# Window attention with a gated convolution: probabilities turned in half-height tiles, the last output block in two column halves, and a new order of the work

## The chip, the cores and the metric

The kernel runs on one core of one Trainium2 chip. A core has a matmul engine (TensorE, in the profile PE, with its weight loads apart as PEld), a vector engine (VectorE, DVE), a scalar engine (ScalarE, ACT), a general engine (GpSimd, POOL) and a queue engine (SyncE, SP) that issues most transfers. The metric is the device time of one execution in microseconds, smaller is better. A profile shows one execution; its span begins and ends with the traced instructions and is a little shorter than the time measured around it.

## The reference

Two layers follow each other. The first is attention with a window of 128 positions and 4 sink positions, on 4 batches, 8 heads, 768 positions and 64 channels per head, all in float32:

```
scores = q @ k.T / sqrt(64)                    # per batch and head, 768 x 768
keep   = (column < 4) | (0 <= row - column < 128)
a      = softmax(where(keep, scores, -1e9))
x      = a @ v                                 # heads put side by side: 4 x 768 x 512
```

The second is a gated convolution over the positions: `gate_pre` is a causal convolution of x with 5 taps per channel, `gate = 1 / (1 + exp(-gate_pre))`, `val = x @ w_val` and `out = (gate * val) @ w_out`, with 512 x 512 weights that arrive as 64-bit floats.

## The kernel before, in words

**Units of work.** The attention is cut into 24 steps. A step is one batch, one third of the positions (two blocks of 128 rows, `p` = 0, 1, 2) and half of the heads (`qd` = 0, 1: two pairs of heads, g = 0, 1, and in a pair the heads j = 0, 1). The second layer is cut into 12 units `m`: one batch and one third of the positions, with all 512 channels; unit m uses steps 2m and 2m+1.

**A step.** `scores` (s0, s1: one per pair of heads) multiplies q and k in 64x32 tiles of the matmul array, 16 matmuls that write a two-bank PSUM tile `pr`; `exps` and `recip` take the softmax, and `normalise` on POOL writes the normalised probabilities to `wx` and the sink columns to the block `skb`, in three parts (high, low, whole) next to each other. The window of a block of 64 queries lies in its own block of 64 keys and the two before it. Half 0 of `wx` ("x") holds the own and the farthest block in one, told apart by a mask when they are copied; half 1 ("y") holds the block between, which needs none. `probs_t` (tx) turns them with 8 transposes of 128x128 into a `pr` tile, a bank for each half; `probs_x` (px) on DVE and `probs_y` (py) on ACT copy them to `wt` in SBUF. `sinks_t` (sk) turns `skb` with one 128x128 transpose into an `ac` tile, `sinks_e` (ts) copies it. `values` (vl) multiplies v and `wt` in 64x64 tiles into `xv`, and `sinks` (si) adds the sinks with two matmuls of 128 rows and 256 columns, one for each pair of heads. There half of the weights `vh` are zero, since each pair's sinks stand in their own half of the rows. Then ACT copies x out (xc, xh), POOL takes the rest (xl) and the first tap (c4), DVE the other four taps (c0, c1), and ACT the tanh (th).

**A unit.** `val` (v0 to v3) is 12 matmuls of 256 columns each; `gated` (g, h, l) multiplies and splits the product in a high and a low part on DVE, ACT and POOL; `outp` (o0 to o3) is 6 matmuls of 512 columns each, two calls per block of 128 output rows; `store` (t0, t1) copies a block on ACT and sends it from SP. All of `val` and `outp` are 128x128 tiles of the array, as the transposes of before are.

**PSUM.** Two tiles `pr` of two banks are passed in turn to scores and turned probabilities, two banks `ac` ("homes") to weights, sinks, `val` and `outp`, and the two banks of `xv` to values.

**Order.** All instructions are issued in a hand-set order: the table `ORDER` names the calls one after the other (`tx.5` is `probs_t` of step 5), and each engine runs its instructions in that order, each held until its operands are there. The matmul engine is filled with work that has no use (`fill`) in the first part, where the weights are decoded from 64 bits (wva to wvf, woa to wof).

## Time and profile before

| | |
|---|---|
| median of 3 runs | 271.12 us (270.26 to 271.2) |
| the profiled execution | 270.55 us, span 268.7 us |
| busy PE / PEld | 258.3 us (96%) / 213.6 us (79%) |
| busy DVE / ACT / POOL | 205.4 (76%) / 189.1 (70%) / 176.2 us (66%) |
| moved by DMA | 36.93 MB, mean 137 GB/s |
| granted PE clock | 0.991 of full speed |

The busy time of an engine is the union of its instructions. A matmul's record is longer than the time for which it keeps the next one waiting, since matmuls run into each other in the array: the distance of two starts is what counts. A float32 matmul that isn't a transpose is recorded as two (`L391 x32` is the 16 matmuls of one `scores` call). Lines are those of the kernel before: L391 scores, L449 turned probabilities, L454 turned sinks, L504 values, L511 sinks, L566 `val`, L606 `outp`.

### The profile page before, as it was taken

The numbers are of one execution on the slowest core, as the hardware profiler recorded it, in microseconds if no ns is written. First come the engines' busy times: TensorE is split into PE (matmuls) and PEld (weight loads), VectorE is DVE, ScalarE is ACT, GpSimd is POOL, SyncE is SP. The second block draws the span as 40 slices with busy tenths as digits, with TensorE's granted clock in tenths as the row PEclk, the third lists the DMA queues.
The fourth block names the chain that finished last, engine by engine and source line by source line (L and its number), as shares of the span: only waits on it lengthen the run. The fifth ranks groups of instructions, "written<-read, shape, count | busy, mean of one in ns | idle before, by whom it ended". The sixth has DMA issues, their size and how long they took to land.

```text
span 268.7 us, 9474 instructions
## 1 busy us (share of the span) xinstructions
PE 258.3 (96%) x3760; PEld 213.6 (79%) x3760; DVE 205.4 (76%) x561; ACT 189.1 (70%) x667; POOL 176.2 (66%) x233
## 2 busy tenths in 40 slices
PE   7899999999999999999999999999999999999990
PEld 3356578789879888879879889889879889898970
DVE  6977989979869878998778788889478857834530
ACT  3899998897888867857676778968567757442420
POOL 6187986876948785675669464895776774816330
PEclk9999999999999999999999999999999999999996
DMA  7998633039344043318833619053335211040202
GB/s 220 370 384 267 239 105 104 0 112 348 107 133 168 1 158 120 131 40 290 262 115 98 196 66 305 3 146 115 111 132 201 59 44 40 1 139 2 78 14 75
DMA packets 27394, 36.93 MB, mean 137 GB/s; under 512 B 2256, under 2 KB 23760, under 8 KB 27344
## 3 DMA queue, kind: packets, MB, share of 16 engines
q1 hardware_dynamic: 26528, 35.48, 39.9%
...
q8 instruction: 31, 0.51, 0.8%
q14 instruction: 19, 0.16, 0.2%
...
## 4 chain that ended last, share of the span: by engine, by line
PE 83%; ACT 9%; POOL 2%; DMA 2%; issue 1%; DVE 0%; POOLq 0%; ACTq 0%
PE ac L606 25%; PE ac L566 25%; PE xv L504 11%; PE pr L391 10%; PE pr L449 7%; ACT w L416 4%; PE xv L511 3%; DMA raw<-in_w_val_dram 2%; PE ac L454 1%; POOL xl L534 1%; ACT wvh L151 1%; ACT wv_p L137 1%; ACT wv_p L156 1%; ACT wvl L183 1%; POOL wo_f L157 0%
## 5 line engine op out<-in xcount | busy, mean ns | idle before, releaser
L547 DVE SCALAR_TENSOR_TENSOR sg<-xv,cw,sg 128x256 f32<-128x256 f32 x192 | 77.8, 474 | 12.4 <-POOL sg L539 7.0
L431 POOL TENSOR_TENSOR wx<-w,sm 128x512 f32<-128x512 f32 x48 | 49.1, 1044 | 11.3 <-DVE sm L423 11.1
L416 ACT ACTIVATE w<-pr,ngm 128x132 f32<-128x132 f32 x136 | 48.5, 369 | 1.7
L595 POOL TENSOR_TENSOR gl<-sg,gh 128x512 fp32r<-128x512 f32 x24 | 31.0, 1295 | 28.1 <-ACT gh L591 28.0
L566 PE MATMUL ac<-xh,wvh 128*128 128x256 f32 x192 | 48.4, 286 | 0.0
L566 PE MATMUL ac<-xh,wvl 128*128 128x256 f32 x192 | 47.1, 279 | 0.0
L606 PE MATMUL ac<-woh,gh 128*128 128x512 f32 x96 | 39.2, 408 | 0.0
L539 POOL TENSOR_TENSOR sg<-xt,cw 128x512 f32<-128x512 f32 x24 | 25.0, 1043 | 20.6 <-ACT xt L518 20.6
L606 PE MATMUL ac<-wol,gh 128*128 128x512 f32 x96 | 38.0, 396 | 0.0
L606 PE MATMUL ac<-woh,gl 128*128 128x512 f32 x96 | 38.0, 395 | 0.0
L566 PEld LDWEIGHTS ac<-xh,wvh 128*128 128x128 f32 x192 | 36.1, 188 | 0.8 <-issue 0.5
L566 PEld LDWEIGHTS ac<-xh,wvl 128*128 128x128 f32 x192 | 36.2, 188 | 0.2
L391 PE MATMUL pr<-k,q 64*32 64x168 f32 x1536 | 35.3, 307 | 0.7 <-DMA q<-in_qt_dram 0.6
L504 PEld LDWEIGHTS xv<-wt,v 64*64 64x64 f32 x1024 | 30.4, 133 | 7.0 <-issue 4.5
L504 PE MATMUL xv<-wt,v 64*64 64x192 f32 (+2 forms) x1024 | 34.5, 278 | 0.2 <-PE ac L566 0.2
L534 POOL TENSOR_TENSOR xl<-xt,xh 128x512 fp32r<-128x512 f32 x24 | 30.8, 1289 | 3.2 <-ACT xh L526 2.8
L566 PE MATMUL ac<-xl,wvh 128*128 128x256 f32 x192 | 30.7, 280 | 0.4 <-POOL xl L534 0.4
L391 PEld LDWEIGHTS pr<-k,q 64*32 64x32 f32 x1536 | 23.8, 106 | 7.9 <-issue 2.6
L396 DVE COPY_PREDICATED pr<-low,pr 128x256 f32<-128x256 uint8 x48 | 20.3, 423 | 12.2 <-PE pr L391 12.2
L591 ACT ACTIVATE gh<-sg 128x512 fp32r<-128x512 f32 x24 | 15.0, 628 | 19.2 <-DVE sg L585 19.2
L416 ACT ACTIVATION_READ_ACCUMULATOR w<-pr,ngm 128x1 f32 x136 | 27.6, 203 | 0.0
L518 ACT ACTIVATE xt<-xv 128x512 f32<-128x512 f32 x24 | 14.4, 600 | 17.3 <-PE xv L511 17.2
...
## 6 DMA issues: line engine op xcount, KB each, us to landing
k<-in_kt_dram SPq DMA_DIRECT2D x23, 408.0 KB, 5.2
v<-in_vt_dram SPq DMA_DIRECT2D x16, 384.0 KB, 4.5
out_dram<-osb SPq DMA_DIRECT2D x24, 256.0 KB, 2.2
q<-in_qt_dram SPq DMA_DIRECT2D x23, 256.0 KB, 5.4
...
v<-in_vt_dram SPq DMA_DIRECT2D x8, 256.0 KB, 5.2
...
```

The costliest lines, as they stand in the source:

```text
L391: nc.tensor.matmul(ss[e * QB:(e + 1) * QB, j, c * n + x0:c * n + x1], q[js, g, (4 * c + e) * QB:(4 * c + e + 1) * QB], k[js, g, (2 * c + e ...
L396: nc.vector.copy_predicated(sv[:, :, :, :D], low[:, None, None, :].to_broadcast([P, 2, 2, D]), sv[:, :, :, 2 * HB:])
L416: nc.scalar.activation(out=w[:, g, j, c], in_=sx[:, j, c, :PK], func=AF.Exp, scale=0.125 if whole else -1.0, bias=ngm[:, g, j, c:c + 1], a ...
L431: nc.gpsimd.tensor_tensor(out=t[:, n].rearrange("p c h x -> p h c x"), in0=w[:, :, :, at], in1=sm.to_broadcast([P, 4, 2, D]), op=ALU.mult)
L449: nc.tensor.transpose(out=x[:, n, o:o + P], identity=ident, in_=ws[s][:, n, c, 2 * g:2 * g + 2].rearrange("p j x -> p (j x)"))
L504: nc.tensor.matmul(acc[o * D:(o + 1) * D, g, x0 + h * D:x0 + (h + a1 - a0 + 1) * D], v[js, g, n], t[js, g, n, a0:a1 + 1].rearrange("p a r ...
L534: nc.gpsimd.tensor_tensor(out=half(xls, s, "xl", F32R), in0=xts[s], in1=half(xhs, s, "xh", F32R).bitcast(F32), op=ALU.subtract)
L539: nc.gpsimd.tensor_tensor(out=half(sg, s, "sg", F32), in0=xts[s], op=ALU.mult, in1=cw[:, g, KT - 1:].to_broadcast([P, 2, PQ]))
L547: nc.vector.scalar_tensor_tensor(out=g, in0=x, scalar=a, in1=g, op0=ALU.mult, op1=ALU.add)
L566: nc.tensor.matmul(acc[:, h], a[:, kc, cs], x[:, kc], start=(n == 0), stop=(n == 11))
L595: nc.gpsimd.tensor_tensor(out=gl, in0=g, in1=gh.bitcast(F32), op=ALU.subtract)
L606: nc.tensor.matmul(acc, a[:, kc, ts], x[:, kc], start=(kc + n == 0), stop=(kc + n == 5))
```

## The change

The transposes of the probabilities are cut in two: each half of the 128 query rows (r = 0, 1) is turned by itself, as 64 rows by 128 columns against a 64x64 identity, and the two halves write different banks. That makes 16 transposes of 64 columns where 8 of 128 stood. `wt` is laid out anew, `probs_y` becomes two ACT instructions (one for each r, 256 elements per partition, or 128 and 256 where p = 0) in place of one of 512 (384), and `probs_x` keeps two DVE instructions of the same size.

The sinks of the two pairs now stand in different halves of `skb`'s columns, 16 for each part, so that `sinks` is two matmuls of 64 rows and 128 columns, one in each half of the array, each to its own bank. The weights `vsk`/`vh` lose their zero half: 64 KB a load in place of 128 KB, and a conversion of 128 elements in place of 256. The subtraction on POOL becomes two of 16 partitions and 128 elements.

In unit 11 the second block of 128 output rows is made in two halves of 256 columns (24 matmuls of 256 in place of 12 of 512), each copied and sent by itself, the first half while the second is being made, in another bank. For units 10 and 11 `outp` collects in a `pr` tile, except for that very last half. `ORDER` is a new table throughout.

```diff
-NR = 8 * NSK
+NR = 4 * NSK
@@ ORDER
-g0.11 th.23 g1.11 h0.11 l0.11 o2.11 h1.11 l1.11 o0.11 o1.11 flag t0.11 o3.11 t1.11
+g0.11 h0.11 l0.11 v3.11 g1.11 h1.11 l1.11 o1.10 t0.10 o0.11 o1.11 o3.10 t0.11 t1.10 flag o2.11 o3.11 t1.11
...
+MP = 10
+LAST = (B * NP - 1, 1)
@@ sink_values
-        vs[b, qd] = h = p2.tile([P, 2, P], F32R, name="vh", tag="vh", bufs=3)
+        vs[b, qd] = h = p2.tile([P, P], F32R, name="vh", tag="vh", bufs=3)
         nc.scalar.activation(out=h, in_=x, func=AF.Copy)
-        r = slice(2 * NR, 3 * NR)
-        nc.gpsimd.tensor_tensor(out=h[r], in0=x[r], in1=h[r].bitcast(F32), op=ALU.subtract)
+        for g in range(2):
+            r = slice(g * D + 2 * NR, g * D + 3 * NR)
+            nc.gpsimd.tensor_tensor(out=h[r], in0=x[r], in1=h[r].bitcast(F32), op=ALU.subtract)
@@ probs_t
-                    o = (2 * g + c) * P
-                    nc.tensor.transpose(out=x[:, n, o:o + P], identity=ident,
-                                        in_=ws[s][:, n, c, 2 * g:2 * g + 2].rearrange("p j x -> p (j x)"))
+                    for r in range(2):
+                        rs, o = slice(r * D, (r + 1) * D), (4 * n + 2 * c + g) * D
+                        nc.tensor.transpose(out=x[:, r, o:o + D], identity=ident[rs, rs],
+                                            in_=ws[s][rs, n, c, 2 * g:2 * g + 2].rearrange("p j x -> p (j x)"))
@@ probs_y
-        nc.scalar.activation(out=t[:, :, 1 + h0:5, 1], in_=x[:, :, h0:], func=AF.Copy)
+        for r in range(2):
+            c = 1 if steps[s][1] + r == 0 else 0
+            nc.scalar.activation(out=t[:, 1 - r, r + c:r + 2, :, 1].rearrange("p k g d -> p (k g) d"),
+                                 in_=x[:, r, 2 * c:], func=AF.Copy)
@@ sinks
         for g in range(2):
-            nc.tensor.matmul(accs[s][:, g, KT - 1:], vs[b, qd][:, g],
-                             skt[s].rearrange("p c r -> p (c r)"), start=False, stop=True, skip_group_check=True)
+            gs = slice(g * D, (g + 1) * D)
+            nc.tensor.matmul(accs[s][:, g, KT - 1:], vs[b, qd][gs], skt[s][gs].rearrange("p c r -> p (c r)"),
+                             start=False, stop=True, skip_group_check=True)
@@ outp
+        if m >= MP:
+            if m not in outs:
+                outs[m] = pair()
+            vacc[m, 2 + i] = outs[m][:, i]
...
+        if (m, i) == LAST:
+            if h:
+                piece(m, i, 0)
+                vacc[m, 2 + i] = acc = homes.pop(0)
+            cs = slice(h * PQ, (h + 1) * PQ)
+            for kc in range(4):
+                for n, (a, x) in enumerate(((gh, wh), (gh, wl), (gl, wh))):
+                    nc.tensor.matmul(acc[:, cs], a[:, kc, ts], x[:, kc, cs], start=(kc + n == 0), stop=(kc + n == 5))
+            return
...
+    def piece(m, i, h):
+        if h == 0:
+            obs[m, i] = p2.tile([P, DM], F32, name="osb", tag="osb", bufs=3)
+        cs = slice(h * PQ, (h + 1) * PQ)
+        nc.scalar.activation(out=obs[m, i][:, cs], in_=vacc[m, 2 + i][:, cs], func=AF.Copy, scale=0.5)
+        at = (2 * (m % NP) + i) * P
+        nc.sync.dma_start(out=out[m // NP, at:at + P, cs], in_=obs[m, i][:, cs])
```

Three places show what the change does to the order. The first is on the matmul engine, at the values of step 5, between two blocks of `outp` and the next scores. Before:

```order
L606 MATMUL ac_92<-wol,gh 128x512
L606 MATMUL ac_92<-woh,gl 128x512
L454 MATMUL ac_93<-ident,skb_108 128x128
L449 MATMUL pr_87<-ident,wx 128x128 x8
L504 MATMUL xv<-wt,v 64x64 x4
L504 MATMUL xv<-wt,v 64x128 x4
L504 MATMUL xv<-wt,v 64x192 x8
L504 MATMUL xv<-wt,v 64x128 x4
L504 MATMUL xv<-wt,v 64x64 x4
L511 MATMUL xv<-skt,vh 128x256 x2
L391 MATMUL pr_86<-k,q 32x168 x16
```

Now (L628 is `outp`, L462 the turned sinks, L454 the turned probabilities, L512 values, L520 sinks, L394 scores):

```order
L628 MATMUL ac_93<-wol,gh 128x512
L628 MATMUL ac_93<-woh,gl 128x512
L462 MATMUL ac_92<-ident,skb_108 128x128
L454 MATMUL pr_87<-ident,wx 128x64 x16
L512 MATMUL xv<-wt,v 64x64 x4
L512 MATMUL xv<-wt,v 64x128 x4
L512 MATMUL xv<-wt,v 64x192 x8
L512 MATMUL xv<-wt,v 64x128 x4
L512 MATMUL xv<-wt,v 64x64 x4
L520 MATMUL xv<-skt,vh 128x256 x2
L394 MATMUL pr_86<-k,q 32x168 x16
```

The sequence of work is the same; the transposes and the sinks have another shape of array tile than `outp` before them, than the values between them, and than the scores behind.

The second is a little later on the same engine, where turned probabilities stand inside a run of `val`. Before:

```order
L566 MATMUL ac_92<-xh,wvl 128x256
L566 MATMUL ac_92<-xl,wvh 128x256 x4
L449 MATMUL pr_86<-ident,wx 128x128 x8
L566 MATMUL ac_93<-xh,wvh 128x256
L566 MATMUL ac_93<-xh,wvl 128x256
```

Now (L575 is `val`):

```order
L575 MATMUL ac_93<-xh,wvl 128x256
L575 MATMUL ac_93<-xl,wvh 128x256 x4
L454 MATMUL pr_86<-ident,wx 128x64 x16
L575 MATMUL ac_92<-xh,wvh 128x256
L575 MATMUL ac_92<-xh,wvl 128x256
```

A run of one tile shape throughout has become three runs.

The third is on POOL in the first part, around the sink values of the first step (`vh`), the decoding of `w_out` (`wo_f`) and the second step's normalisation. Before:

```order
L438 TENSOR_TENSOR skb_107<-skb_107 128x32
L157 TENSOR_TENSOR wo_f<-wo_e,wo_p 128x512
L259 TENSOR_TENSOR vh<-vs,vh 32x256
L431 TENSOR_TENSOR wx<-w,sm 128x4x2x64 x2
L434 TENSOR_TENSOR skb_108<-w,sm 128x32
```

Now:

```order
L442 TENSOR_TENSOR skb_107<-skb_107 128x2x16
L262 TENSOR_TENSOR vh<-vs,vh 16x128 x2
L159 TENSOR_TENSOR wo_f<-wo_e,wo_p 128x512
L434 TENSOR_TENSOR wx<-w,sm 128x4x2x64 x2
L438 TENSOR_TENSOR skb_108<-w,sm 128x2x16
```

The sink values are two instructions and stand ahead of the decoding; the rest keeps its place.

More of the change, by code (lines that the diff above doesn't have):

```diff
@@ L77 @@
-ts.23 v2.10 v3.10 g0.10 c4.22 hd.22 c0.22 c1.22 th.21 g1.10 h0.10 l0.10 o2.10 vv.23 vl.23 h1.10 si.23 xc.23
-hd.23 xh.23 l1.10 xl.22 o0.10 o1.10 c4.23 c0.23 xl.23 t0.10 c1.23 o3.10 v0.11 th.22 v1.11 t1.10 v2.11 v3.11
-g0.11 th.23 g1.11 h0.11 l0.11 o2.11 h1.11 l1.11 o0.11 o1.11 flag t0.11 o3.11 t1.11
+fill.5 masks load_conv wvl.0 kq.0 signs leads conv_weights wva.0 wvb.0 wvd.0 s0.0 wvc.0 wvl.1 wva.1 wvl.2
+blanks e0.0 s1.0 wva.2 e1.0 wvb.1 wvc.1 fill.10 wve.0 wvf.0 wvb.2 wvc.2 kq.1 s1.1 wol.0 rec.0 norm.0 kq.2 e1.1
@@ new lines @@
+wvd.1 vv.0 woa.0 s0.1 e0.1 fill.7 wvl.3 s1.2 sv.0 e1.2 wve.1 fill.4 wol.2 wob.0 woc.0 kq.3 tx.0 px.0 py.0
+fill.6 sk.0 rec.1 norm.1 s0.2 ts.0 kq.4 wod.0 vl.0 woe.0 wva.3 e0.2 wvb.3 wvf.1 si.0 s0.3 xc.0 c4.0 rec.2
+wvc.3 tx.1 xh.0 wvd.3 hd.0 fill.6 wvd.2 kq.6 px.1 wof.0 wve.2 wol.1 c0.0 e0.3 c1.0 norm.2 vv.1 py.1 woa.1
+wve.3 wvf.3 wol.3 sv.1 wob.1 tx.2 py.2 px.2 s1.3 xl.0 sk.1 ts.1 wvf.2 vv.2 vv.3 vl.1 si.1 sk.2 wod.1 xc.1 c4.1
+ts.2 hd.1 s0.4 kq.7 woc.1 woe.1 xh.1 xl.1 c0.1 e1.3 rec.3 norm.3 c1.1 th.0 woa.3 wob.3 e0.4 v0.0 v1.0 y0.0
@@ L247, in load_v @@
         if p == 0:
-            vraw[b, qd] = x = p2.tile([P, 2, P], F32, name="vs", tag="vs", bufs=2)
+            vraw[b, qd] = x = p2.tile([P, P], F32, name="vs", tag="vs", bufs=2)
             nc.sync.dma_start(out=x, in_=vsk[b, qd])
@@ L432, in normalise @@
                                     in1=sm.to_broadcast([P, 4, 2, D]), op=ALU.mult)
-        sk = [skb[s % 2][:, n * NR:(n + 1) * NR] for n in range(3)]
-        nc.gpsimd.tensor_tensor(out=sk[0].rearrange("p (h c n) -> p h c n", c=2, n=NSK), in0=w[:, :, :, D:HB],
-                                in1=sm.to_broadcast([P, 4, 2, NSK]), op=ALU.mult)
+        sk = [skb[s % 2].rearrange("p (g k r) -> p k g r", g=2, r=NR)[:, n] for n in range(3)]
+        w, sm = (x.rearrange("p g j c x -> p g (j c) x") for x in (wn[s][0], wn[s][2][:, :, :, :, None]))
+        nc.gpsimd.tensor_tensor(out=sk[0].rearrange("p g (h n) -> p g h n", n=NSK), in0=w[:, :, :, D:HB],
+                                in1=sm.to_broadcast([P, 2, 4, NSK]), op=ALU.mult)
         nc.gpsimd.tensor_scalar(out=sk[2].bitcast(F32R), in0=sk[0], scalar1=1.0, scalar2=None, op0=ALU.mult)
@@ L469, in prob @@
         if s not in probs:
-            probs[s] = p2.tile([P, 2, 6, 3, D], F32, name="wt", tag="wt", bufs=2)
+            probs[s] = p2.tile([P, 2, 3, 2, 3, D], F32, name="wt", tag="wt", bufs=2)
         return probs[s]
     def probs_x(s):
-        h0 = 2 if steps[s][1] == 0 else 0
-        t = prob(s)
-        x = trs[s][:, 0].rearrange("p (g h r) -> p g h r", g=2, r=D)
-        nc.vector.tensor_tensor(out=t[:, :, 2:6, 0], in0=x, in1=cur[:, None, None, :].to_broadcast([P, 2, 4, D]),
-                                op=ALU.mult)
-        nc.vector.tensor_tensor(out=t[:, :, h0:4, 2], in0=x[:, :, h0:],
-                                in1=prev[:, None, None, :].to_broadcast([P, 2, 4 - h0, D]), op=ALU.mult)
-    def probs_y(s):
-        h0 = 1 if steps[s][1] == 0 else 0
-        t = prob(s)
-        x = trs[s][:, 1].rearrange("p (g h r) -> p g h r", g=2, r=D)
-        nc.scalar.activation(out=t[:, :, 1 + h0:5, 1], in_=x[:, :, h0:], func=AF.Copy)
+        c0 = 1 if steps[s][1] == 0 else 0
+        t, x = prob(s), turned(s, 0)
+        for k, c, a, m in ((1, 0, 0, cur), (c0, c0, 2, prev)):
+            nc.vector.tensor_tensor(out=t[:, :, k:k + 2 - c, :, a].rearrange("p r k g d -> p r (k g) d"),
+                                    in0=x[:, :, 2 * c:], op=ALU.mult,
+                                    in1=m[:, None, None, :].to_broadcast([P, 2, 4 - 2 * c, D]))
+    def probs_y(s):
+        t, x = prob(s), turned(s, 1)
+        for r in range(2):
+            c = 1 if steps[s][1] + r == 0 else 0
+            nc.scalar.activation(out=t[:, 1 - r, r + c:r + 2, :, 1].rearrange("p k g d -> p (k g) d"),
+                                 in_=x[:, r, 2 * c:], func=AF.Copy)
     xhs, xls, sg, accs = {}, {}, {}, {}
@@ L599, in outp @@
         gh, gl = gs[m]
-        if h == 0:
+        if m >= MP:
+            if m not in outs:
+                outs[m] = pair()
+            vacc[m, 2 + i] = outs[m][:, i]
+        elif h == 0:
             vacc[m, 2 + i] = homes.pop(0)
```

93 lines of the change are left out of this document (48 added, 45 removed).

## The prediction

> **What bounds the kernel now.** I read the page's first parts, then the busy time by stretches, then the chain that ended last.
>
> ```profile
> PE 258.3 (96%) x3760; PEld 213.6 (79%) x3760; DVE 205.4 (76%) x561; ACT 189.1 (70%) x667; POOL 176.2 (66%) x233
> ...
> PE 83%; ACT 9%; POOL 2%; DMA 2%; issue 1%; DVE 0%; POOLq 0%; ACTq 0%
> ```
>
> The stretches (start:end, length, busy time of each engine with its instructions, granted clock, DMA share, GB/s):
>
> ```profile
> 0.00:38.80 38.80, 35.68 (x465) 19.99 (x465) 31.55 (x95) 33.26 (x118) 28.17 (x52) 1.00 0.80 274
> 37.10:261.75 224.65, 223.98 (x3306) 194.70 (x3304) 175.13 (x470) 156.88 (x558) 149.67 (x183) 1.00 0.36 116
> ```
>
> From the first `val` at 37.1 us to the last matmul, PE is idle for 224.65 - 223.98 = 0.67 us in all, at full clock, and DVE, the next engine, is busy for 78% of it. So 224.65 us are the sum of PE's own work, and what a change does there is the change in that work. Ahead of it the chain runs over ACT and then POOL, and behind it over the last copy and store:
>
> ```profile
> 33.08 0.86 POOL vh L259
> 34.03 1.27 POOL xl L534
> 35.30 1.23 POOL wo_f L157
> 36.53 1.00 POOL sg L539
> 37.53 1.26 POOL xl L534
> 38.84 1.92 PE ac L566 x14
> ...
> 261.75 0.60 ACT osb L610
> ```
>
> **What PE pays for a tile shape.** The view is PE's instructions in order of time (start, duration, form). The distance of two starts is the cost.
>
> ```profile
> 57.49 0.80 PE L391 MATMUL pr<-k,q 64*32 64x168 f32 x32
> 58.23 1.09 PE L449 MATMUL pr<-ident,wx 128*128 128x128 f32 x8
> ...
> 67.17 1.37 PE L391 MATMUL pr<-k,q 64*32 64x168 f32 x64
> 68.47 0.50 PE L511 MATMUL xv<-skt,vh 128*128 128x256 f32 x2
> 68.81 0.39 PE L606 MATMUL ac<-woh,gh 128*128 128x512 f32 x1
> 69.04 0.39 PE L606 MATMUL ac<-wol,gh 128*128 128x512 f32 x1
> ...
> 71.60 1.04 PE L449 MATMUL pr<-ident,wx 128*128 128x128 f32 x8
> 72.39 0.48 PE L606 MATMUL ac<-woh,gh 128*128 128x512 f32 x1
> 72.71 0.39 PE L606 MATMUL ac<-wol,gh 128*128 128x512 f32 x1
> ...
> 75.37 1.04 PE L449 MATMUL pr<-ident,wx 128*128 128x128 f32 x8
> 76.34 1.55 PE L504 MATMUL xv<-wt,v 64*64 64x64 f32 x48
> 77.81 0.38 PE L511 MATMUL xv<-skt,vh 128*128 128x256 f32 x1
> ```
>
> Two matmuls of `outp` start 0.23 us apart for 512 columns, which makes 0.117 for 256. Eight transposes and the `outp` matmul behind them take 72.71 - 71.60 = 1.11, so the transposes take 0.87, 0.109 each. Now the borders. Two scores calls in a row take 1.30, one alone 58.23 - 57.49 = 0.74: a call in the stream costs 0.56, and leaving its 64x32 tiles costs about 0.16. Transposes before values take 76.34 - 75.37 = 0.97, so leaving 128x128 costs 0.10. The two sinks matmuls take 68.81 - 68.47 = 0.34 although 2 x 0.117 = 0.23 is their own: entering 128x128 costs another 0.10. So every run of one tile shape, whatever is in it, costs 0.16 to 0.20 at its two ends together. In a sentence beside it: the Trainium skill, "TensorEngine Tiling (Array Packing)", section "Tiling Modes" with its Key Properties, says that changing the tiling mode, not just the tile, drains the engine; the trace agrees, with these 0.10 to 0.16 us at an end, and the rule speaks against this change.
>
> The forms, with mean ns:
>
> ```profile
> L449 PE MATMUL pr<-ident,wx 128*128 128x128 f32 x192 | 25.2, 274 | 0.3 <-ACT w L416 0.3
> L449 PEld LDWEIGHTS pr<-ident,wx 128*128 128x128 f32 x192 | 21.7, 141 | 2.8 <-POOL wx L431 0.9 <-issue 0.8
> L391 PEld LDWEIGHTS pr<-k,q 64*32 64x32 f32 x1536 | 23.8, 106 | 7.9 <-issue 2.6 <-DMA q<-in_qt_dram 1.5 <-ACT sm L422 0.7
> L504 PEld LDWEIGHTS xv<-wt,v 64*64 64x64 f32 x1024 | 30.4, 133 | 7.0 <-issue 4.5 <-PE ac L606 0.6 <-ACT wt L486 0.6
> L504 PE MATMUL xv<-wt,v 64*64 64x64 f32 x320 | 12.6, 227 | 0.2 <-PE ac L566 0.2
> ```
>
> **The transposes.** 16 of 64 columns replace 8 of 128. Do the two half-height tiles run side by side? Values do: 48 records in four tiles take 1.47 us, 0.031 each, while one record lasts 0.227 or more; and a load of 64 columns, which by the step from 106 ns (32 columns) to 133 ns (64) keeps its path for about 2 x 27 = 54 ns, would need 48 x 0.054 = 2.6 us one after the other. So loads, too, run side by side in different tiles. A pair of half-height transposes then costs the longer of two things. Streaming: 0.109 / 2 = 0.055. The load: 128 columns still, whose record of 141 ns lies 62 ns over the 79 that are left of the 32-column load without its columns (106 - 27). I take 0.062, 8 x 0.062 = 0.50 in place of 0.87: 0.37 saved. Ends: 0.44 (streaming alone) to 0.87 (a pair costs what one transpose does now). From the first `val` on, 21 of the 24 steps turn their probabilities (168 of the 192 transposes): **21 x 0.37 = -7.8 us** (-9.0 to 0).
>
> **The sinks.** Two matmuls of 256 columns side by side in place of one after the other: -0.117, for the 22 steps whose sinks come after the first `val`: **-2.6 us** (0 if they don't overlap).
>
> **The new borders.** Counted in the order of PE from the first `val` on, runs of one shape go from 79 (31 of 128x128, 26 of 64x32, 22 of 64x64) to 116: 35, 26, 22, and 33 of the new 64x128. Four more of the first kind at 0.10 + 0.10: +0.8. The 33 new ones have no row; scores' 0.16 is the nearest, with ends of 0.10 (one side of the wide shape) and 0.20. I take 0.17: 33 x 0.17 = +5.6 (3.3 to 6.6). **Together +6.4 us**. This gives back more than half of what the halves save: where transposes stand inside `val`, as in the second place shown, 0.37 are saved and 0.17 + 0.20 paid.
>
> **The first part.** The copies and the sink values, in these rows:
>
> ```profile
> L486 ACT ACTIVATE wt<-pr 128x512 f32<-128x512 f32 x16 | 9.6, 598 | 4.8 <-PE pr L449 2.9 <-DVE wt L479 1.4 <-PE ac L606 0.5
> L486 ACT ACTIVATE wt<-pr 128x384 f32<-128x384 f32 x8 | 4.0, 494 | 0.9 <-PE pr L449 0.5 <-DVE wt L479 0.2
> L462 ACT ACTIVATE skt<-ac,blk 128x128 fp32r<-128x128 f32 x12 | 3.8, 382 | 0.0
> L257 ACT ACTIVATE vh<-vs 128x256 fp32r<-128x256 f32 x8 | 3.3, 418 | 0.5 <-DMA vs<-in_vsk_dram 0.5
> L259 POOL TENSOR_TENSOR vh<-vs,vh 32x256 fp32r<-32x256 f32 x8 | 6.2, 779 | 2.6 <-ACT ngm L413 1.8 <-POOL gl L595 0.2 <-POOL sg L539 0.2
> L438 POOL TENSOR_TENSOR skb<-skb 128x32 f32<-128x32 f32 x24 | 7.2, 299 | 2.0
> ```
>
> A copy of 256 elements is about 0.42, so two in place of one of 512 add 2 x 0.418 - 0.598 = 0.24 per step; 24 x 0.24 = 5.7 us on ACT, which has 224.65 - 156.88 = 68 us idle in the long stretch. There it is hidden; without that cover it would be 5 us. In the first part it isn't: three copies come before the first `val` (0.382 + 0.418 - 0.494 = 0.31 twice, 0.24 once, by whole records, which overlap), and the two smaller `vh` give 2 x 0.04 back, 0.8 at most. On POOL a subtraction of 128 elements lies between the 32 of L438 and the 256 of L259, near 0.30 + 0.48 x 96/224 = 0.51, so two are 1.01 in place of 0.78; two steps have it on the chain above, +0.46. The new order puts the first ahead of `wo_f`, which it then delays by about 1.0, and the reset of `skb` behind the first decoding. The two engines follow each other on the chain, so the ends are 0 and 0.8 + 0.46 = 1.3; I take **+0.5 us**.
>
> **The end.** The last copy has 256 elements in place of 512 and the last store 128 KB in place of 256:
>
> ```profile
> L610 ACT ACTIVATE osb<-ac 128x512 f32<-128x512 f32 x24 | 14.2, 595 | 13.0 <-PE ac L606 13.0
> ...
> SPq L781 <- SPq L781: 4.0, 1, 4.0
> ```
>
> -0.18 for the copy (595 to about 418); of the 4.0 us for which SP waits at the end, half the bytes may take off some tenths, between 0 and 0.4. **-0.4 us** for both. 24 matmuls of 256 columns cost PE the same as 12 of 512 (24 x 0.117 = 12 x 0.23). I cost the `pr` tiles for units 10 and 11 at nothing: the last scores and transposes are over by then. The loads keep their lead over PE:
>
> ```profile
> k<-in_kt_dram SPq DMA_DIRECT2D x23, 408.0 KB, 5.2
> v<-in_vt_dram SPq DMA_DIRECT2D x16, 384.0 KB, 4.5
> q<-in_qt_dram SPq DMA_DIRECT2D x23, 256.0 KB, 5.4
> ```
>
> The last column is the median time to landing. By the PE durations above, laid along the new order, the shortest time from the last use of a buffer to the next need is 7.6 us for k and q and 6.6 for v.
>
> **Sum.** -7.8 - 2.6 + 6.4 + 0.5 - 0.4 = -3.9 against the profiled execution's 270.55 us: 266.65. The median of the runs is 271.12, 0.57 above it, so the forecast is **267.2 us**. With the ends of the two large unknowns (-9.0 and 3.3; 0.20 a border) the forecast's own range is 263.5 to 269.5.
>
> **Rivals.** About 0.5%, 1.36 us, is what a measurement of this kernel can tell from no change: faster is below 269.8, slower above 272.5.
>
> ```profile
> L566 PEld LDWEIGHTS ac<-xh,wvh 128*128 128x128 f32 x192 | 36.1, 188 | 0.8 <-issue 0.5
> ```
>
> A, slower: the weight load sets the pace of the half-height transposes. Place: the 16 loads of each turned step, still 128 columns each. For it: nothing in the trace shows a 64-row load of 128 columns, and the 0.109 of a transpose could be its load as well as its streaming. Against it: the load's record is 141 ns, not the 188 of a `val` load of as many columns, in the row above. If a pair costs 0.109, the 7.8 are gone: -2.6 + 6.4 + 0.5 - 0.4 = +3.9, a median of 275.0. The two tiles one after the other at 0.055 give the same. It decides from 0.086 a pair on, where 21 x (0.87 - 8 x 0.086) = 3.9. Beside it stands the Trainium skill, "TensorE: Matmul & The Clock Gate", section "LDWEIGHTS (loading the stationary operand)": a load takes its columns / 1.2 ns, however few its rows. By that, as an estimate from the page, a pair costs 0.107, the sum is about +3.6 and the time 274.7; the 62 ns worked out above disagree, but no row here shows them alone.
>
> B, no change: PE waits. With less work of its own it comes sooner to the values, whose `wt` now needs two ACT copies, 0.24 longer, behind a queue that runs in order. The L504 row above has 0.6 us of waits for ACT's `wt` ahead of the values' loads, so the lead is thin at places. 0.15 in each of 21 steps is +3.2: 270.4.
>
> C, faster still: a border between two shapes of the same height (64x64 to 64x128, 20 of them from the first `val` on) needs no drain. Then 20 x 0.16 = 3.2 less: 264.0. Scores before values, both 64 high, leave 0.16 as well, which speaks against it.
>
> **Chances.** Forecast 0.52, A 0.18, B 0.16, C 0.14. Faster = forecast and C, 0.66; the same = B, 0.16; slower = A, 0.18. The range reaches to C's 262.5 below and to the near part of A, 274.0, above; some 0.16 is left out.
>
> **What would show it.** Right: PE still without idle time from about 37.5 us on, ending near 257.5; L454 with x16 taking near 0.5 us plus a border, L520 0.12 plus a border and 0.10 before the next wide matmul; distances of 0.14 to 0.20 at the new borders. Wrong: 16 transposes in 0.9 us or more (A); idle time of PE in front of L512 with ACT `wt` as releaser (B); the first `val` after 38.5; sinks starting right behind values (C).

## The result and the profile after

The changed kernel takes **266.12 us** (median of 4 runs, 265.92 to 266.28), the kernel before beside it on the same chip 270.84 us (4 runs, 270.26 to 271.2): a ratio of **0.9827, 95% interval 0.9806 to 0.9849**. The profiled executions are 266.28 and 270.55 us, the spans 264.1 and 268.7. It is faster, by 4.7 us; the forecast was 267.2, with 263.5 to 269.5 as its own range. Here and below, a median is over all executions, a ratio over those within 1.5% of the fastest one of their kernel.

First the page's busy times of the kernel after, then its busy time by stretches (columns as in the prediction), cut at the first `val` and at the last matmul:

```profile
PE 254.5 (96%) x3960; PEld 205.4 (78%) x3964; DVE 206.4 (78%) x561; ACT 188.6 (71%) x692; POOL 177.3 (67%) x241
```

```profile
0.00:37.97 37.97, 34.61 (x476) 18.00 (x480) 31.97 (x94) 32.62 (x119) 27.64 (x54) 1.00 0.85 287
37.97:258.35 220.38, 219.88 (x3486) 187.41 (x3484) 174.48 (x468) 155.56 (x574) 149.71 (x188) 1.00 0.36 115
```

In the long stretch PE is idle for 220.38 - 219.88 = 0.50 us, so it is still the sum of PE's own work, and that sum is smaller. By the starts of matmuls, the span divides as follows:

| us | before | after | difference | forecast |
|---|---|---|---|---|
| up to the first `val` | 37.14 | 37.97 | +0.83 | +0.5 |
| first `val` to last matmul | 224.13 | 220.15 | -3.98 | -4.0 |
| last matmul to the end | 7.43 | 6.00 | -1.43 | -0.4 |

The 0.83 is less than it looks: before, a wait of 0.36 us for `xl` stood just inside `val`, and after it doesn't. The 1.43 comes from one trace of each kernel, and further down it turns out that such ends vary. The middle row is made of these kinds (each matmul's distance to the next start, summed by kind; leaving a shape counts to the kind that is left):

| us | turned probabilities | sinks | turned sinks | `outp` | `val` | scores | values |
|---|---|---|---|---|---|---|---|
| before | 17.61 | 7.75 | 2.53 | 68.92 | 70.27 | 26.54 | 30.52 |
| after | 12.89 | 6.13 | 3.60 | 70.06 | 70.53 | 26.42 | 30.51 |

Turning and sinks give 6.3 us, and 2.5 of them come back where `outp`, `val` and the turned sinks are now entered and left more often. These are PE's instructions of the kernel after in order of time (L394 scores, L454 turned probabilities, L462 turned sinks, L512 values, L520 sinks, L575 `val`, L628 `outp`):

```profile
46.09 0.39 PE L520 MATMUL xv<-skt,vh 64*128 64x256 f32 x2
46.32 0.66 PE L454 MATMUL pr<-ident,wx 64*128 64x64 f32 x16
...
66.64 1.37 PE L394 MATMUL pr<-k,q 64*32 64x168 f32 x64
67.94 0.38 PE L520 MATMUL xv<-skt,vh 64*128 64x256 f32 x2
68.25 0.50 PE L628 MATMUL ac<-woh,gh 128*128 128x512 f32 x1
...
71.25 0.72 PE L454 MATMUL pr<-ident,wx 64*128 64x64 f32 x16
71.89 0.51 PE L628 MATMUL ac<-woh,gh 128*128 128x512 f32 x1
...
190.97 0.39 PE L520 MATMUL xv<-skt,vh 64*128 64x256 f32 x2
191.19 0.66 PE L454 MATMUL pr<-ident,wx 64*128 64x64 f32 x16
191.78 0.50 PE L628 MATMUL ac<-woh,gh 128*128 128x512 f32 x1
...
224.64 0.39 PE L520 MATMUL xv<-skt,vh 64*128 64x256 f32 x2
224.86 1.16 PE L454 MATMUL pr<-ident,wx 64*128 64x64 f32 x32
225.95 0.49 PE L628 MATMUL ac<-woh,gh 128*128 128x512 f32 x1
```

**Transposes.** The comparison has to be between calls with the same neighbours. Behind sinks, which have their shape, and ahead of `outp`, 32 take 225.95 - 224.86 = 1.09 us and 16 take 191.78 - 191.19 = 0.59. So 16 in the stream cost 1.09 - 0.59 = 0.50, where 8 of the old ones cost 0.872: **0.37 saved a step**. That is 0.062 a pair, and the trace has the starts of the pairs inside the calls 0.060 to 0.065 apart; only the first pair behind sinks is followed after 0.055. **Borders.** Behind `outp` the same 16 take 71.89 - 71.25 = 0.64: 0.05 more for the way in, with 0.11 from the first pair to the second, and from the last pair on it is 0.15 in place of 0.06, so 0.09 is the way out. The sinks show the same way out: followed by transposes of the same shape they take 46.32 - 46.09 = 0.23, followed by `outp` 68.25 - 67.94 = 0.31. Of the 0.23 only 0.117 is the work of one 256-column matmul, so 0.11 is their way in. A run of the new shape costs 0.14 us at its two ends when it begins with transposes, and 0.20 when it begins with sinks. The two sinks start 3 ns apart in the trace, where the kernel before started the second 0.12 to 0.22 us behind the first: they do run side by side. Scores to sinks, 67.94 - 66.64 = 1.30, is what two scores calls cost ahead of a 128x128 shape before.

The forms, which the prediction gave for the kernel before:

```profile
L454 PE MATMUL pr<-ident,wx 64*128 64x64 f32 x384 | 16.4, 226 | 0.2 <-POOL wx L434 0.2
L454 PEld LDWEIGHTS pr<-ident,wx 64*128 64x128 f32 x384 | 14.1, 139 | 4.5 <-issue 1.3 <-POOL wx L434 1.0 <-POOL skb L442 0.6
L512 PEld LDWEIGHTS xv<-wt,v 64*64 64x64 f32 x1024 | 30.3, 133 | 6.3 <-issue 3.3 <-PE ac L628 0.6 <-ACT wt L493 0.6
L520 PE MATMUL xv<-skt,vh 64*128 64x256 f32 x48 | 9.5, 383 | 0.0
```

The load of a half-height transpose has a record of 139 ns, the old one of 141: halving the rows changes nothing in the record. The idle time ahead of the values' loads is the 0.6 us for ACT's `wt` that stood there before, so the second ACT copy made no new wait.

### The profile page after: what moved, and what is told of

Same layout as the page of the kernel before. It is cut to its first block, busy times and chain, and to the rows that moved or that the text cites. A ratio compares the mean times of both kernels' runs of the same rounds, so it can differ in the third digit from the quotient of the medians.

```text
span 264.1 us, 9936 instructions
## 1 busy us (share of the span) xinstructions
PE 254.5 (96%) x3960; PEld 205.4 (78%) x3964; DVE 206.4 (78%) x561; ACT 188.6 (71%) x692; POOL 177.3 (67%) x241
## 4 chain that ended last, share of the span: by engine, by line
PE 81%; DMA 2%; POOL 2%; ACT 2%; issue 1%; SPq 0%
PE ac L575 24%; PE ac L628 22%; PE xv L512 12%; PE pr L394 10%; PE pr L454 4%; PE pr L628 3%; PE xv L520 3%; DMA q<-in_qt_dram 2%; PE ac L462 1%; ACT w L419 1%; PE ac L624 1%; PE pr L624 1%; POOL wo_f L159 0%; POOL vh L262 0%; POOL xl L543 0%
## 5 line engine op out<-in xcount | busy, mean ns | idle before, releaser
L575 PE MATMUL ac<-xh,wvh 128*128 128x256 f32 x192 | 48.9, 289 | 0.0
L575 PE MATMUL ac<-xh,wvl 128*128 128x256 f32 x192 | 47.1, 279 | 0.0
L575 PEld LDWEIGHTS ac<-xh,wvh 128*128 128x128 f32 x192 | 36.3, 189 | 1.7 <-issue 0.5
L394 PE MATMUL pr<-k,q 64*32 64x168 f32 x1536 | 35.5, 307 | 1.0 <-DMA q<-in_qt_dram 0.5
L575 PEld LDWEIGHTS ac<-xh,wvl 128*128 128x128 f32 x192 | 36.2, 188 | 0.2
L512 PEld LDWEIGHTS xv<-wt,v 64*64 64x64 f32 x1024 | 30.3, 133 | 6.3 <-issue 3.3
L512 PE MATMUL xv<-wt,v 64*64 64x192 f32 (+2 forms) x1024 | 34.5, 278 | 0.2 <-ACT wt L493 0.2
L628 PE MATMUL ac<-woh,gh 128*128 128x512 f32 x80 | 33.1, 414 | 0.0
L628 PE MATMUL ac<-woh,gl 128*128 128x512 f32 x80 | 31.8, 397 | 0.0
L628 PE MATMUL ac<-wol,gh 128*128 128x512 f32 x80 | 31.7, 396 | 0.0
L394 PEld LDWEIGHTS pr<-k,q 64*32 64x32 f32 x1536 | 23.8, 106 | 8.8 <-issue 3.2
L575 PE MATMUL ac<-xl,wvh 128*128 128x256 f32 x192 | 30.5, 280 | 0.0
L575 PEld LDWEIGHTS ac<-xl,wvh 128*128 128x128 f32 x192 | 25.9, 188 | 0.2 <-POOL xl L543 0.2
```

Source lines behind the costliest of these rows:

```text
L394: nc.tensor.matmul(ss[e * QB:(e + 1) * QB, j, c * n + x0:c * n + x1], q[js, g, (4 * c + e) * QB:(4 * c + e + 1) * QB], k[js, g, (2 * c + e ...
L512: nc.tensor.matmul(acc[o * D:(o + 1) * D, g, x0 + h * D:x0 + (h + a1 - a0 + 1) * D], v[js, g, n], t[js, n % 2, n // 2, g, a0:a1 + 1].rearr ...
L575: nc.tensor.matmul(acc[:, h], a[:, kc, cs], x[:, kc], start=(n == 0), stop=(n == 11))
L628: nc.tensor.matmul(acc, a[:, kc, ts], x[:, kc], start=(kc + n == 0), stop=(kc + n == 5))
```

## The experiments

Each row is timed beside the kernel before on the same chip; ratios are to it.

| kernel | us (runs) | ratio [interval] | first `val` to last matmul, PE idle in it |
|---|---|---|---|
| after | 266.12 (4) | 0.9827 [0.9806, 0.9849] | 220.15, 0.51 |
| tiles_old_order | 272.84 (10) | 1.0046 [1.0001, 1.0092] | 225.72, 4.03 |
| turns_only | 273.39 (4; 268.82 to 274.19) | - | - |
| sinks_only | 272.83 (10) | 1.0066 [1.0039, 1.0093] | 226.68, 2.05 |
| no_tail | 266.40 (4) | 0.9834 [0.9786, 0.9882] | 219.83, 0.35 |
| early_loads | 269.54 (12) | 0.9954 [0.9927, 0.9982] | 222.99, 1.77 |
| merged | 270.60 (12) | 0.9991 [0.9975, 1.0007] | 225.44, 5.99 |
| old_turns | 270.47 (10) | 0.9982 [0.9969, 0.9996] | 224.80, 0.00 |
| old_sinks | 267.92 (4) | 0.9887 [0.9866, 0.9908] | 222.84, 1.03 |
| half_turns | 265.56 (4) | 0.9793 [0.9767, 0.9819] | 220.31, 0.12 |
| xl_first | 267.34 (6) | 0.9856 [0.9834, 0.9879] | 220.05, 0.43 |
| low_later | 265.83 (5) | 0.9826 [0.9801, 0.9851] | 221.10, 0.83 |

### The new tiles without the new order

The changed kernel with the table of the kernel before, without the split of the last block and with `outp` in its old banks:

```diff
 ORDER = """
-fill.5 masks load_conv wvl.0 kq.0 signs leads ...
+blanks wvl.0 load_conv kq.0 masks signs leads fill.5 ...
-MP = 10
+MP = 99
-LAST = (B * NP - 1, 1)
+LAST = None
```

> The half-height transposes and sinks in the order of before, without the split of the last block and without the scores' banks for units 10 and 11. Theory (borders between tile shapes cost 0.16 to 0.20 us, a turned step saves 0.43): from the first val on 121 runs of one shape in place of 79, so 21 x 0.43 + 22 x 0.117 = 11.6 saved and 42 x 0.20 = 8.4 paid, about -3.2, with +0.5 ahead of the first val: 268.0 to 268.6 against 270.8. Rival (the gain of the change is that of the new order, not of the tiles): 270.5 or more. Rival (with the old order PE runs into waits that the new order takes away): PE idle time of 2 us or more after the first val, and 270 or more.

It missed by more than 4 us: 272.84, slower than before if anything, and the last rival's idle time is there, 4.03 us. (The expectation's 0.43 a step, 0.06 too much, as shown above, is 21 x 0.06 = 1.3 us of the miss.) The trace says where. PE in order of time, then the stretches around it:

```profile
129.96 1.36 PE L394 MATMUL pr<-k,q 64*32 64x168 f32 x60
134.02 0.48 PE L394 MATMUL pr<-k,q 64*32 64x168 f32 x4 [2.70 <-issue]
134.42 0.39 PE L520 MATMUL xv<-skt,vh 64*128 64x256 f32 x2
```

```profile
116.00:121.00 5.00, 5.00 (x94) 3.91 (x92) 4.71 (x17) 2.27 (x5) 4.21 (x7) 1.00 0.16 56
121.00:126.00 5.00, 5.00 (x64) 4.86 (x57) 4.19 (x13) 3.96 (x14) 3.61 (x6) 1.00 0.89 278
126.00:131.00 5.00, 5.00 (x138) 4.64 (x139) 3.29 (x8) 3.70 (x16) 2.63 (x3) 1.00 1.05 351
131.00:134.02 3.02, 0.32 (x20) 0.01 (x1) 1.01 (x2) 0.00 (x0) 1.02 (x3) 1.00 0.23 74
```

PE stops after 60 of 64 scores matmuls, in the middle of one call, whose operands are all there, and "issue" says that it waits for nothing that the profile names. The page lists a DMA queue of kind "instruction":

```profile
q8 instruction: 33, 0.54, 0.9%
```

That is 16 KB a packet (0.54 MB / 33), and packets come about every 256 of PE's instructions, matmuls and weight loads together. By the trace's records of this queue around the halt:

```
kernel            fetch before     next fetch       PE instructions between
before            113.97-114.85    124.35-125.24    265
tiles_old_order   118.31-119.95    131.52-132.62    550
turns_only        118.99-119.92    131.28-132.40    522
```

The halt ends 1.4 us after the late fetch. Between the two, SP had issued eleven loads in a row (v, k, q, k, q, v, vs, v, vs, k, q at 121.16 to 126.41), which kept the DMA engines at 278 and then 351 GB/s until 131.3. Theory formed here: PE's next block of instructions stood behind that burst, and PE ran out of what it had. The Trainium skill, "Runtime: NRT & Kernel Launch", section "Instruction fetch mechanics", has the blocks of 256 instructions over a DMA queue and calls the cost of a block's end mostly hidden; the packets of 16 KB agree, and this 3.0 us halt is a case where it isn't hidden.

### One part alone, in the old order

`turns_only` has only the new transposes, `sinks_only` only the new sinks, both in the table of before.

```diff
 # turns_only: as tiles_old_order, with the sinks of before
-            nc.tensor.matmul(accs[s][:, g, KT - 1:], vs[b, qd][gs], skt[s][gs].rearrange("p c r -> p (c r)"),
+            nc.tensor.matmul(accs[s][:, g, KT - 1:], vs[b, qd][:, g], skt[s].rearrange("p c r -> p (c r)"),
 # sinks_only: as tiles_old_order, with the transposes of before
-                    for r in range(2):
-                        ... identity=ident[rs, rs] ...
+                    nc.tensor.transpose(out=x[:, n, o:o + P], identity=ident, ...)
```

> Of the change only the half-height transposes of the probabilities, in the order of before. Theory: 21 x 0.43 = 9.0 saved from the first val on, and 115 runs of one shape in place of 79, 36 x 0.20 = 7.2 paid: -1.8, so 268.5 to 269.7. Rival (borders are free): 262. Rival (the load sets the pace): slower than 275.

> Of the change only the sinks in two 64x128 tiles, in the order of before. Theory: each of 22 pairs saves 0.117 on PE, and stands alone between other shapes, so 99 runs of one shape in place of 79: -2.6 + 20 x 0.20 = +1.4, and up to +0.5 for the split subtraction on POOL ahead of the first val: 271.5 to 273, slower than before. Rival (a border between two shapes of the same height costs nothing, or the drain was there before): 268 to 269, faster.

`sinks_only` came out where expected, 272.83, but only in part for the reason expected. The stretch from the first `val` to the last matmul is 2.55 us longer than before. 1.1 of it is PE's own work: the pairs save 2.6, and 20 more runs of a shape (99 against 79) cost 3.7, 0.18 each. The rest is idle time, and 1.25 of it one halt in the middle of a scores call, like the one above:

```profile
67.67 1.07 PE L394 MATMUL pr<-k,q 64*32 64x168 f32 x45
70.00 0.76 PE L394 MATMUL pr<-k,q 64*32 64x168 f32 x19 [1.25 <-issue]
```

Here the fetch came 374 instructions after the last one, at 67.54, with the loads at over 300 GB/s until then. `turns_only` gave one execution of 268.82, in the range expected, and three of 273.09 to 274.19. Its profile is of one of the three; there is none of the fast one, so what sets that one apart is inferred. PE stops behind the same 60 matmuls of the same call as in `tiles_old_order`, here for 2.6 us, and behind the halt stand these stretches, the last with

```profile
126.00:131.00 5.00, 5.00 (x131) 4.67 (x132) 3.33 (x7) 4.04 (x16) 2.46 (x3) 1.00 1.05 361
131.00:135.00 4.00, 1.71 (x37) 1.06 (x22) 1.73 (x4) 0.20 (x1) 1.06 (x2) 1.00 0.18 56
135.00:140.00 5.00, 5.00 (x17) 3.94 (x16) 4.16 (x11) 4.78 (x23) 2.59 (x3) 0.66 0.46 138
```

a granted clock (the column ahead of the DMA share) of 0.66. In the records of the clock it is 0.50 for 3.41 us from 135.06 on, right after 3.41 us in which PE was busy for 1.22. There the matmuls of `outp` start 0.43 us apart, in place of 0.23, so by these numbers a PE that is busy throughout loses up to 1.7 us. Half a clock for 3.41 us is 0.006 of the mean clock of an execution, and the three long ones have 0.985 to 0.987 where the fast one has 0.993. The ten executions of `tiles_old_order` part the same way: the five with a mean clock of 0.985 to 0.987 took 273.4 to 273.8, the five at 0.993 or 0.994 269.6 to 272.3.

### The burst of loads taken apart

`tiles_old_order` with three of the calls that load moved up, by 9 to 38 calls:

```diff
 ORDER (of the kernel before)
-... c4.9 c0.9 t1.3 o0.3 ... xl.9 vv.11 norm.11 ... norm.12 kq.15 tx.11 ... l0.4 kq.14 tx.12 ...
+... c4.9 c0.9 vv.11 kq.15 kq.14 t1.3 o0.3 ... xl.9 norm.11 ... norm.12 tx.11 ... l0.4 tx.12 ...
```

> The tiles of the change in the order of before, as in the run before, with three loads (v of step 11, k and q of steps 15 and 14) issued ahead of the two stores of unit 3 in place of behind them, so that the ten loads that came within 6 us at 121 to 127 us are spread. Theory (PE ran out of instructions at 131.0 us because the fetch of its next 256 stood behind those loads, and the halt then lowered its clock): no halt near 131 us, all runs between 267.5 and 268.8. Rival (the order of before keeps PE waiting whatever the loads do): a halt of 2 us or more stays, 270 or more.

269.54, 3.3 us under `tiles_old_order` (2.5 by the two ratios), and above the range expected: ten of the twelve executions took longer than 268.8. The long halt is gone (the longest distance of two matmuls is 0.94 us), and six loads, not eleven, stand in the burst:

```profile
121.00:126.00 5.00, 5.00 (x76) 4.85 (x69) 4.18 (x16) 3.43 (x11) 3.25 (x4) 1.00 0.82 246
126.00:131.00 5.00, 5.00 (x117) 4.66 (x118) 3.68 (x8) 4.11 (x18) 2.45 (x4) 1.00 0.23 79
```

The fetch that came at 131.52 now comes at 127.15, again just as the loads run dry, and PE still has instructions then: 281 since the last one. By these two kernels the halt hangs on how long the loads keep the DMA engines full after a fetch. That the fetch *waited* behind the loads is inferred from these times in both kernels; no record shows it queued. 3.1 us still lie between this kernel and `no_tail`, which has the same tiles in the new order: 1.77 - 0.35 = 1.4 of them idle time of PE, and 1.0 by five runs of one shape more (121 against 116) at 0.20; the remaining 0.7 are not accounted for.

### Parts undone in the new order

```diff
 # no_tail
-LAST = (B * NP - 1, 1)
+LAST = None
 # old_turns: probs_t, prob, probs_x, probs_y and values as before; old_sinks: NR = 8 * NSK,
 # load_v, sink_values, normalise, sinks and the layout of vsk as before
```

> The changed kernel with the last block of unit 11 made, copied and sent whole, as before. Theory (the forecast's term): 0.4 us slower than the changed kernel, 266.5. Rival (the traces of the two kernels: 7.4 us from the last matmul's start to the end before, 6.0 after): 1.4 slower, 267.5. If the last store lands 4 us after its issue here too, it is its size; if it lands in 2 to 2.5 us, what was seen before was another transfer in its way.

> The changed kernel with the 128x128 transposes of before, all else as changed. Theory: 21 x 0.43 = 9.0 us more matmul work from the first val on, and 102 runs of one shape in place of 116, 2.8 less: +6.2, 272.3. Rival (the new order is worth most of the gain): 268 or less.

> The changed kernel with the 128x128 sinks of before, all else as changed. Theory: 22 x 0.117 = 2.6 us more, and as many runs of one shape (116: 13 more of 128x128, 13 fewer of 64x128): 268.7. Rival (the sinks gain nothing, as by themselves in the order of before): 266.1.

`no_tail`: 266.40 against 266.12, so the split of the last block is worth 0.28 us, and the intervals don't tell it from nothing. Its way from the last matmul to the end is 6.58 us, that of the changed kernel 6.00 and that of the kernel before 7.43. So 0.85 of the 1.43 gained there come with whole blocks too: from the end of the last copy to the end of the span it took 6.35 us before and 5.5 in `no_tail`, for the same 256 KB. What makes that difference is open, and one trace of a kernel is thin for it: the five kernels with the old order, all with a whole last block, have 6.82 to 7.44 us from the last matmul to the end, the seven with the split 5.61 to 6.37.

`old_turns`: 270.47, so in the new order the half-height transposes are worth **4.35 us**, less than the 6.2 expected. The expectation's 0.43 a step was the error: 21 x 0.37 = 7.8, less 14 runs of a shape at 0.17 to 0.20, is 5.0 to 5.4, and PE's own work differs by 224.80 - (220.15 - 0.51) = 5.2; half a microsecond of idle time, which only the changed kernel has, goes the other way. `old_sinks`: 267.92, so the sinks are worth **1.8 us** here, where they were a loss without the new transposes. The count of runs tells why: 116 with the new sinks and 116 with the old ones. 9 of the 22 stand right ahead of transposes that now have their shape, so what the new shape costs at some places it saves at others, and of the 2.6 PE's own work keeps 2.2 ((222.84 - 1.03) against (220.15 - 0.51)).

### Fewer borders still

If a border costs 0.20, then five runs fewer should be worth 1.0 us. Four transposes were moved next to sinks or other transposes:

```diff
 ORDER
-... sk.5 ts.5 tx.6 py.6 px.6 t0.1 vl.5 si.5 xc.5 ...
+... sk.5 ts.5 t0.1 vl.5 si.5 tx.6 xc.5 px.6 py.6 ...
 (and tx.8 behind si.7, tx.21 behind si.20, tx.17 behind tx.18)
```

> The changed kernel with the turned probabilities of steps 6, 8 and 21 moved behind the sinks that stand next to them (5, 7, 20), and those of step 17 next to those of step 18: 111 runs of one tile shape from the first val on in place of 116. Theory (a border costs, whatever stands there): five runs at 0.20 us fewer, 1.0 us less: 265.1. Rival (the copies that come later make PE wait for the values): 266.1 or more, with PE idle ahead of the values of steps 6, 8, 17 or 21.

Missed: 270.60, no gain over the kernel before. PE's own work did fall, by 0.2 us only, and 5.5 us of idle time came in. (A matmul's record is longer than its distance to the next, so a wait of a tenth or two hides in the tail of a record and counts as work; how much of the other 0.8 is of this kind was not separated.) The view of waits by form (its last part names what ended the idle time ahead of the group; L352 are scores, L412 transposes, L470 values in this kernel):

```profile
L352 PE MATMUL pr<-k,q 64*32 64x168 f32 x1536 | 35.7, 307 | 4.3 <-ACT wt L451 2.2 <-DMA q<-in_qt_dram 1.2 <-ACT w L377 0.6
L412 PE MATMUL pr<-ident,wx 64*128 64x64 f32 x384 | 16.2, 225 | 2.3 <-ACT xv L497 1.2 <-POOL skb L400 0.9 <-POOL wx L392 0.2
...
L470 PE MATMUL xv<-wt,v 64*64 64x64 f32 x320 | 12.6, 227 | 0.9 <-DVE sg L514 0.8
```

```profile
77.74 0.33 PE L420 MATMUL ac<-ident,skb 128*128 128x128 f32 x1
78.84 0.80 PE L352 MATMUL pr<-k,q 64*32 64x168 f32 x32 [0.78 <-ACT wt L451]
```

A transpose that is moved back holds its `pr` tile until ACT has made `wt` of it, and the next scores wait for that tile. So at such places the other engines' lead over PE is smaller than the delay, and a border saves 0.20 at most.

### Side by side?

The changed kernel with half of its transposes left out:

```diff
-                    for r in range(2):
+                    for r in range(1):
```

> The changed kernel with half of the transposes of the probabilities left out (those of the first 64 rows remain; the other half of the turned probabilities is then whatever lay in the bank, and part of the computation is missing). Theory (two half-height transposes run side by side, on different rows of the PE): a step's 8 remaining ones take as long as its 16 did, so PE needs 12.9 us for them as before and the time stays where the changed kernel has it, 266.1 us (265.6 to 266.6); in the trace two calls in a row take about 1.09 us and one 0.64. Rival (they run one after the other, each 0.028 us): half of the 0.44 us that a call costs falls away, 21 x 0.22 = 4.6 us, and the time is 261.5 us.

265.56, against 266.12; the first `val` to the last matmul is 220.31 against 220.15. PE in order of time:

```profile
71.01 0.71 PE L454 MATMUL pr<-ident,wx 64*128 64x64 f32 x8
71.65 0.50 PE L628 MATMUL ac<-woh,gh 128*128 128x512 f32 x1
...
224.81 1.15 PE L454 MATMUL pr<-ident,wx 64*128 64x64 f32 x16
225.90 0.50 PE L628 MATMUL ac<-woh,gh 128*128 128x512 f32 x1
```

Eight take 0.64 us where sixteen took 0.64, and sixteen 1.09 where thirty-two did. The second half of the transposes is free: two of them, on different rows of the array and into different banks, run side by side. This settles it. The trace shows one thing more: the transposes of one half alone start 0.060 to 0.065 us apart as well, so the 0.062 of a pair doesn't come from the two halves getting in each other's way.

### An earlier start: two tries to beat both

In the changed kernel PE waits just ahead of the first `val`:

```profile
36.14 0.79 PE L181 MATMUL ac<-woh,minus 128*128 128x512 f32 x1
37.63 0.50 PE L182 MATMUL ac<-wo_f,plus 128*128 128x512 f32 x1 [0.70 <-POOL wo_f L159]
37.97 0.28 PE L575 MATMUL ac<-xh,wvh 128*128 128x256 f32 x1
```

```diff
 ORDER
-... wvf.3 wol.3 sv.1 wob.1 ... s1.3 xl.0 sk.1 ...
+... wvf.3 wol.3 xl.0 sv.1 wob.1 ... s1.3 sk.1 ...
```

> The changed kernel, in whose order POOL makes the low part of the first gated input (`xl`, 128x512) ahead of the low rows of the second batch pair's sinks (`vh`, two of 16x128) instead of behind them. In the changed kernel POOL waits at 31.8 us for ACT's `vh`, and `xl`, `sg` and `wo_f` follow it in a row up to the first of the `val` matmuls at 37.97 us. Theory (that row sets the start of `val`, and PE has no idle time behind it): POOL gains the wait and the two small ones, 0.8 to 1.4 us, the first `val` starts at 36.6 to 37.2 us, and the time is 265.1 us (264.7 to 265.4). Rival (something else is ready only then: a load, or PE's own work ahead of it): the first `val` stays at 37.9 us and the time at 266.1 us.

Missed, on the far side of the rival: 267.34, and the first `val` at 40.03 in the profiled execution. The subtraction `xl` did start earlier on POOL; beside it, this is what became of DVE's shift for the output weights (first line POOL, second DVE, both of `xl_first`):

```profile
32.03 1.27 POOL L543 TENSOR_TENSOR xl<-xt,xh 128x512 fp32r<-128x512 f32 x1
```

```profile
32.12 1.46 DVE L142 TENSOR_SCALAR wo_t<-wo_p 128x512 int32<-128x512 int32 x1
```

and the same instruction in the changed kernel, with POOL idle beside it:

```profile
31.84 0.43 DVE L142 TENSOR_SCALAR wo_t<-wo_p 128x512 int32<-128x512 int32 x1
```

1.46 us in place of 0.43. The extra 1.03 is nearly the 1.18 that POOL's instruction still had to run when DVE's started. The changed kernel has three more such meetings, where this shift takes 1.07, 0.83 and 0.97 us while a POOL product of two inputs still has 0.79, 0.54 and 0.68 to run: in all four, what was left of POOL's instruction and 0.28. The Trainium skill, "SBUF — State Buffer", section "Who interferes with whom", says that a DVE instruction in a two-port mode and a GpSimd one exclude each other, and that whoever starts first holds the ports for its whole instruction; these times agree, though no row shows the mode in which the shift ran. DVE's `wt` is late by it, so scores start at 36.30 in place of 34.84, and behind that wait stands another drop of the clock. The stretches of `xl_first`:

```profile
36.00:37.31 1.31, 1.01 (x33) 0.50 (x33) 1.28 (x3) 1.31 (x5) 0.98 (x1) 0.76 0.94 275
37.31:39.61 2.30, 2.30 (x9) 1.17 (x5) 2.15 (x6) 2.23 (x12) 2.30 (x3) 0.50 0.09 31
```

The records of the clock have 0.50 from 36.69 for 3.41 us, after 3.41 us in which matmuls kept PE busy for 2.17. Of the 2.06 us by which the first `val` is later, 1.46 are the late scores.

The second try leaves POOL and DVE where they are to each other, and moves what PE waits for behind `val`:

```diff
 ORDER
-... s0.4 kq.7 woc.1 woe.1 xh.1 xl.1 c0.1 ... v0.0 v1.0 y0.0
+... s0.4 kq.7 woe.1 xh.1 xl.1 woc.1 c0.1 ... v0.0 v1.0 wog.1 y0.0
 # woe.1 issues the first two matmuls of the weight's sum, wog.1 the third, on wo_f
```

> The changed kernel with three things moved ahead of the first `val`: the third matmul of the second output-weight column (the one on `wo_f`, for which PE waits 0.70 us at 36.9) goes behind the first two `val` blocks, the second half of `xh` and `xl` goes ahead of the copy and the product that make `wo_f`, and nothing is put beside DVE's bit operations that was not there before. Theory (the start of `val` is set by what PE waits for there, and the run of the kernel before this one, xl_first, lost its gain because POOL's 128x512 subtraction and DVE's `wo_t` held each other up): `xl` is ready at about 37.9 us, the first `val` starts at 36.7 to 37.0 instead of 37.97, the moved matmul costs 0.25 to 0.35 later, and the time is 265.4 us (265.1 to 265.8). Rival (the output weights made later delay the decoding behind them, which shares ACT, POOL and a bank): the gain comes back as idle time of PE within 20 us, and the time is 266.1 us or more.

265.83: inside neither account, and at the same ratio to the kernel before as the changed kernel (0.9826 against 0.9827), so no gain that can be measured. The first `val` did start at 37.20 in place of 37.97, and it was given back within 4 us:

```profile
40.00 0.40 PE L184 MATMUL ac<-wo_f,plus 128*128 128x512 f32 x1
40.99 1.55 PE L514 MATMUL xv<-wt,v 64*64 64x64 f32 x48 [0.59 <-PE ac L184]
```

```profile
39.28 1.61 DVE L558 SCALAR_TENSOR_TENSOR sg<-xv,cw,sg 128x256 f32<-128x256 f32 x4
```

The values that follow start at 40.99, in the changed kernel at 40.86. PE's own matmul, which the view names, can't be what they wait for; DVE's convolution reads the bank `xv` that they write, and ends at 40.89. By these times the next thing to set the start stands right behind the first, and none of the runs beats the changed kernel.

## Why the prediction was right

The forecast of 267.2 is 1.1 us above the time. Mechanism, sign, the bound and the three terms of PE's own work hold; the two ends of the kernel were off, in opposite directions. 0.7 of the 1.1 is the step from the profiled execution to the median, +0.57 in the forecast and -0.16 (266.28 to 266.12) as measured, which is the scatter of executions. The range holds the time, but its upper end is wider than the ends that the sum names: they make 267.2 - 1.2 - 2.3 = 263.7 and 267.2 + 1.0 = 268.2. The four chances add up to 1.00 as they stand, so the 0.16 that is said to be left out has no place among them.

- **What bounds it.** Right: PE without idle time from the first `val` on (0.51 us), the sum being PE's own work.
- **Transposes, forecast -7.8.** Measured 21 x (0.872 - 0.50) = -7.8. The working took a pair's cost as the longer of two things, the streaming's 0.055 and the load's 0.062, and the pairs come every 0.062. That the load is what sets it is likely, but no run changed the load alone.
- **Sinks, forecast -2.6.** As worked out: started 3 ns apart, 0.117 saved a pair.
- **Borders, forecast +6.4.** The whole stretch moved by -3.98; with -7.8 and -2.6 taken out, 6.4 us are left for 37 more runs of a shape, 0.17 each. By the same count 42 more runs cost 0.20 each in `tiles_old_order`, 20 more 0.18 in `sinks_only`, and 14 fewer save 0.19 in `old_turns`. The working had 0.17 for the 33 new runs from scores' 0.16, as the nearest row, and the two kinds of run that it holds measured 0.14 and 0.20. That their mean came out there, so that the -4.0 agrees to 0.02, is luck in part.
- **First part, forecast +0.5.** +0.83 by the first `val`, +0.47 with the wait for `xl` that before had behind it. The start of the first decode, DVE's first `wv_t`, lies anywhere from 5.94 to 6.86 us in these runs; counted from there, the first `val` comes after 30.65 us before, after 31.56 in the changed kernel and 31.5 in `no_tail`, `merged` and `half_turns`, so the +0.8 is no accident of one trace. PE waits 0.70 us for POOL's `wo_f` there, as the working had it.
- **The end, forecast -0.4.** -1.43 in the traces. The split alone is worth 0.28 by the medians of `no_tail`; in its trace the end is 0.58 longer and the stretch ahead of it 0.32 shorter. That fits the part that the working costed; the other 0.85 lies in how long the last store took before. The working gave it nothing, and its cause is open.
- **Rival A** (the load sets the pace, or the two tiles run one after the other) is refuted twice: 0.062 a pair, where it would have decided from 0.086 on, and `half_turns`, where half of the transposes save nothing. **Rival C** is refuted by the 0.15 that values still pay on their way to 64x128, as in the kernel before. **Rival B** is not in the changed kernel (0.2 us of PE's idle time ahead of values goes to ACT's `wt`). Its price was too high as well: ACT's copies of `wt` are busy for 15.0 us in all, in place of 13.5, so two copies take 0.06 a step longer than one and not 0.24. But it is what `merged` ran into, with 2.2 us for `wt` ahead of scores and 5.99 of idle time in all.

What the prediction did not see is how much of the result hangs on the new order. It read the order for borders and for the loads' lead, and found no term in it. With the same tiles the old order takes 272.84 us, 6.4 more than `no_tail` (5.7 by the ratios): 3.3 (2.5) went with `early_loads`, that is with the burst of loads and, by the account above, with PE's late instructions and the clock's drop behind them; of the rest, 1.4 are other idle time and 1.0 borders. None of the rivals had the first: a burst of loads was looked at for the lead of its own data, not for the instructions that PE has to be sent meanwhile.
